# Three plain blocks of a fused attention and MoE kernel: one after the other, in an order laid out by a list scheduler

## The chip, the cores and the metric

The kernel runs on one core of a Trainium2 chip. The metric is the device time of one execution in microseconds, and kernels are compared by the median of several runs. A profile of one execution is at hand beside it; its span runs from the first to the last recorded instruction.

## The reference, cut to what matters

Attention is local: the sequence of 576 is cut into 9 chunks of 64, and each chunk of each of 8 heads and 8 batches attends to itself alone. The result goes through a two-layer network with a gate between the layers, for all 4608 tokens.

```python
scores = scale * np.matmul(q_c, k_c.transpose(0, 1, 2, 4, 3))
attn = np.exp(scores - np.max(scores, axis=-1, keepdims=True))
attn = attn / (np.sum(attn, axis=-1, keepdims=True) + 1e-09)
x = np.matmul(attn, v_c)                     # laid out as (4608, 512)
h = x @ w_in                                 # (512, 2048)
g = h * np.clip(h + 3.0, 0.0, 6.0) / 6.0
out = g @ w_out                              # (2048, 512)
```

## The kernel before, in words

The 4608 tokens are cut into nine blocks of 512. A block's attention is done in two halves, called heads here: head 01 is block 0, second half. A head loads qk (1 MB) and v (0.5 MB), and then takes these steps: scores (TensorE, 64 small products, L158), the maximum (VectorE, L165), its subtraction (L168), exp (ScalarE, L169), the sum and its inverse (VectorE, L172 to L174), the division (L176), transpose (TensorE, L187), its copy (ScalarE, L189), the product with v (TensorE, L198), and then the block's operand x. To keep float32 accuracy at the faster fp32r rate, each operand is split in a high part (a ScalarE cast, L207) and a low part (a VectorE subtraction, L210), and each product is made of three: high by high, high by low, low by high (L225, L226, L227). Every such product has 512 columns.

The 2048 hidden features are cut into 16 tiles, ft. A tile has 12 products in the first layer (mm1, into the PSUM tile h, of which there are two), a gate on ScalarE and VectorE that yields the tile g with its high and low part (L237 to L240), and 12 products in the second layer (mm2, into four accumulators acc). mm2 runs two tiles behind mm1 (LAG). So a tile of a block is 24 products.

The weights come as 64-bit words, one tile of 1 MB each, and have to be converted first: two ScalarE passes (L111, L114), a shift and a join on VectorE (L112, L115), a ScalarE cast to the high part (L119) and a VectorE subtraction for the low part (L120). The loads are issued on SyncE's queue (L99), at most three tiles ahead of the conversion.

Three blocks, 0 to 2, run in this plain way. The other six run in three pairs with seven products of sums in the place of eight (the pair phase, with tiles named xop and ws); its weight sums are made during the plain phase from the converted weights, in 16 units of four steps (`prepare`, L338 to L367), and stored in DRAM. The first operands of the pair phase (`x_operands`) are made at the end of the plain phase.

The order of the plain phase is written by hand. SEGMENTS (L29) says which tiles follow which: tiles 0 to 3 of block 0, then all 16 of block 1, then tiles 4 to 15 of block 0, then block 2. Between its two segments the sums of block 0 are copied out of the accumulators into `part` tiles (parked, L268 and L270), and added to the second segment's sums at its end (L262 to L266, some on GpSimd). Two slots per tile are counted, and attention steps and sum units are tied to slots by hand (`plan`). Until slot 26 (SUMS) the instructions are put in order by the framework's own scheduler, with some hints (`issue_after`); from there on each engine's instructions keep the order in which the code gives them (`manual_schedule`). Before the first products there are fillers on TensorE, products of no use that keep it busy: 11 at the start and then 36, 6 and 4 at fixed places (WARM, WARM2).

Each engine runs its instructions in the order given to it and waits at each for the semaphores of what it needs.

Of the kernel before, what the change touches and what calls it, by code (L numbers as in the profile page):

```python
# [28 lines left out]
SEGMENTS = [(0, 0, 4), (1, 0, 16), (0, 4, 16), (2, 0, 16)]  # L29
# [7 lines left out]
WARM2 = (0, 36, 0, 6, 4)  # L37
LAG = 2
EDGE = 32


@with_exitstack
def tile_kernel(ctx: ExitStack, tc: tile.TileContext, qk_in, v_in, weights, out):
# [49 lines left out]
    loaded = converted = 0  # L93

    def load_to(ft):
        nonlocal loaded
        while loaded < min(ft, NFT):
            t = w_tile(loaded, I32).rearrange("p l m t -> p (l m t)")
            nc.sync.dma_start(out=t.rearrange("p (m t) -> p m t", m=2), in_=weights[loaded].bitcast(I32).rearrange("m p t -> p m t"))  # L99
            words[loaded] = t.rearrange("p (n t) -> p n t", t=2)  # L100
            loaded += 1

    def convert(ft):

        u = wsc.tile([P, 1024], I32, name="u")
        r = wsc.tile([P, 1024], I32, name="r")
        lo, hi = words[ft][:, :, 0], words[ft][:, :, 1]

        ACT.activation(out=u.bitcast(F32), in_=hi.bitcast(F32), func=AF.Prelu, scale=2.0 ** -112, alpha=2.0 ** 32)  # L111
        DVE.tensor_scalar(out=u, in0=u, scalar1=3, scalar2=None, op0=ALU.logical_shift_left)  # L112

        ACT.activation(out=r, in_=lo.bitcast(U32), func=AF.Copy, scale=2.0 ** -29)  # L114
        DVE.tensor_tensor(out=u, in0=u, in1=r, op=ALU.add)  # L115
        a = u.bitcast(F32).rearrange("p (m t) -> p m t", m=2)
        w[ft] = w_tile(ft, F32R)
        w_h[ft], w_l[ft] = w[ft][:, 0], w[ft][:, 1]
        ACT.copy(out=w_h[ft], in_=a)  # L119
        DVE.tensor_tensor(out=w_l[ft], in0=a, in1=w_h[ft].bitcast(F32), op=ALU.subtract)  # L120

    def convert_to(ft):
        nonlocal converted
        load_to(ft + 3)
        while converted < min(ft, NFT):
            convert(converted)
            converted += 1
# [4 lines left out]
    class Attention:  # L132
# [6 lines left out]
        def load(self, qk=None, v=None):  # L139
            self.load_qk(qk)  # L140
            self.load_v(v)

        def load_qk(self, qk=None):

            self.qk = qk or ap.tile([P, 2, NB, 2 * CH], F32, name="qk")
            return nc.sync.dma_start(out=self.qk.rearrange("p a c t -> p (a c t)"), in_=qk_in[self.n, self.dp])
# [13 lines left out]
        def soft(self, step, e=None):  # L160
            flat = lambda t: t.rearrange("p a c t -> p (a c) t")
            wide = lambda t: t.unsqueeze(2).broadcast_to([P, 2 * NB, CH])
            if step == 0:
                self.m = small.tile([P, 2 * NB], F32, name="m")
                DVE.tensor_reduce(out=self.m, in_=flat(self.s), axis=AX.X, op=ALU.max)  # L165
            elif step == 1:
                self.e = e if e is not None else ap.tile([P, 2, NB, CH], F32, name="e")
                DVE.tensor_tensor(out=flat(self.e), in0=flat(self.s), in1=wide(self.m), op=ALU.subtract)  # L168
                ACT.activation(out=flat(self.e), in_=flat(self.e), func=AF.Exp, scale=SCALE)  # L169
            elif step == 2:  # L170
                self.z = small.tile([P, 2 * NB], F32, name="z")
                DVE.tensor_reduce(out=self.z, in_=flat(self.e), axis=AX.X, op=ALU.add)  # L172
                DVE.tensor_scalar_add(out=self.z, in0=self.z, scalar1=1e-9)
                DVE.reciprocal(out=self.z, in_=self.z)  # L174
            else:
                self.done = DVE.tensor_tensor(out=flat(self.e), in0=flat(self.e), in1=wide(self.z), op=ALU.mult)  # L176

        def softmax(self, e=None):
            for step in range(4):
                self.soft(step, e)  # L180

        def transpose(self):

            tp = self.psum().rearrange("p a (i t) -> p a i t", t=P)
            for a in range(2):
                for i in range(NB // 2):
                    PE.transpose(out=tp[:, a, i], in_=self.e[:, a, 2 * i:2 * i + 2].rearrange("p c t -> p (c t)"), identity=ident)  # L187
            self.aT = self.e.rearrange("p a c t -> p (a c t)").rearrange("p (a i t) -> p a i t", a=2, t=P)
            ACT.copy(out=self.aT, in_=tp)  # L189

        def values(self):

# [6 lines left out]
            src = po.rearrange("p s a i t -> p s (a i) t")  # L199
            as_src = lambda t: t.rearrange("p a (i s t) -> p s (a i) t", s=2, t=CH)  # L200
            if self.n >= NSTD:
                if self.n not in xraw:
                    xraw[self.n] = raw.tile([P, NDP, 2, NT], F32, name="x")
                ACT.copy(out=as_src(xraw[self.n][:, self.dp]), in_=src)
                return
# [8 lines left out]

    xraw = {}
    xs = {}
    low = []

    def finish():
        while low:  # L220
            low.pop(0)()
# [256 lines left out]
    for _ in made:  # L478
        pass
# [200 lines left out]
```

## Time and profile before

| What | us |
|---|---|
| median of three runs | 822.61 (822.45 to 823.38) |
| the profiled execution | 823.05 |
| its span | 821.0 |
| TensorE products busy | 800.5 |
| VectorE busy | 620.3 |
| ScalarE busy | 367.2 |
| GpSimd busy | 131.6 |

The granted clock of TensorE is 1.00 on average. Engines: PE is TensorE (products), PEld its weight loads, DVE VectorE, ACT ScalarE, POOL GpSimd, SP SyncE. A line L225 is line 225 of the kernel before. In the table by stretches each row has the stretch, its length, and for PE, PEld, DVE, ACT and POOL the busy time with the count of instructions in brackets; then the granted clock, the busy share of the DMA engines and GB/s. The rows for one tile have no POOL column. In the timeline a row is start, duration, engine, line, operation, tiles and count, and in brackets how long the engine was idle before and who ended that. In the groups a row is line, engine, operation, tiles and shapes, count, then busy time, mean in ns, and the idle time before with its releasers. In the list of waits a row is who waited for whom, total us, times and the longest. Products overlap, and their recorded length (390 ns) is longer than their spacing.

### The profile page before, as it was taken

The numbers are of one execution on the slowest core, as the hardware profiler recorded it, in microseconds if no ns is written. First come the engines' busy times: TensorE is split into PE (matmuls) and PEld (weight loads), VectorE is DVE, ScalarE is ACT, GpSimd is POOL, SyncE is SP. The second block draws the span as 40 slices with busy tenths as digits, with TensorE's granted clock in tenths as the row PEclk, the third lists the DMA queues.
The fourth block names the chain that finished last, engine by engine and source line by source line (L and its number), as shares of the span: only waits on it lengthen the run. The fifth ranks groups of instructions, "written<-read, shape, count | busy, mean of one in ns | idle before, by whom it ended". The sixth has DMA issues, their size and how long they took to land.

```text
span 821.0 us, 13680 instructions
## 1 busy us (share of the span) xinstructions
PE 800.5 (98%) x5683; PEld 650.2 (79%) x5683; DVE 620.3 (76%) x753; ACT 367.2 (45%) x455; POOL 131.6 (16%) x78
## 2 busy tenths in 40 slices
PE   7889999999999999999999999999999999999998
PEld 5667888888878888788788887888788887878886
DVE  5869978877787864876989667778898566679951
ACT  4858934443444443443474432344634423337330
POOL 0000000000010000212271031222440312227100
PEclk9999999999999999999999999999999999999999
DMA  9883026677685761665656667566555664555573
GB/s 367 326 339 150 1 76 220 209 253 244 195 294 173 259 249 52 232 222 198 234 187 228 231 240 257 194 216 246 187 198 203 227 212 180 190 206 188 185 230 129
DMA packets 50158, 172.86 MB, mean 211 GB/s; under 512 B 4656, under 2 KB 17200, under 8 KB 39344
## 3 DMA queue, kind: packets, MB, share of 16 engines
q1 hardware_dynamic: 49952, 171.85, 59.7%
q8 instruction: 45, 0.74, 0.3%
q10 hardware_dynamic: 144, 0.13, 0.0%
q14 instruction: 17, 0.14, 0.0%
HBM read 133.17 MB, written 38.80 MB: 209 GB/s over the span
## 4 chain that ended last, share of the span: by engine, by line
PE 75%; DVE 13%; ACT 5%; issue 3%; DMA 2%; SPq 1%; POOL 0%; DVEq 0%; ACTq 0%
PE acc L225 16%; PE acc L226 16%; PE acc L227 16%; PE h L225 8%; PE h L227 8%; PE h L226 8%; DVE xop L384 2%; PE two L198 2%; DMA w<-w_in_out 1%; DVE g L508 1%; PE two L187 1%; DVE u L496 1%; PE two L158 1%; DVE e L168 1%; ACT r L507 1%
## 5 line engine op out<-in xcount | busy, mean ns | idle before, releaser
L225 PE MATMUL acc<-xop,ws 128*128 128x512 f32 x528 | 208.4, 395 | 4.5 <-DVE u L496 4.5
L226 PE MATMUL acc<-xop,ws 128*128 128x512 f32 x528 | 205.8, 390 | 0.0
L227 PE MATMUL acc<-xop,ws 128*128 128x512 f32 x528 | 205.2, 390 | 0.0
L225 PEld LDWEIGHTS acc<-xop,ws 128*128 128x128 f32 x528 | 99.1, 188 | 27.7 <-DVE u L496 6.9
L384 DVE TENSOR_TENSOR xop<-g,xop 128x1024 fp32r<-128x1024 f32 x72 | 103.4, 1468 | 21.5 <-ACT xop L383 21.5
L227 PEld LDWEIGHTS acc<-xop,ws 128*128 128x128 f32 x528 | 99.1, 188 | 20.9
L226 PEld LDWEIGHTS acc<-xop,ws 128*128 128x128 f32 x528 | 99.2, 188 | 19.7
L383 ACT CAST xop<-g 128x1024 fp32r<-128x1024 f32 x72 | 74.6, 1054 | 78.6 <-PE acc L227 52.8
L516 POOL TENSOR_TENSOR g<-g 128x512 f32<-128x512 f32 x24 | 34.7, 1448 | 300.8 <-DVE g L508 300.8
L225 PE MATMUL h<-x,w 128*128 128x512 f32 x192 | 75.7, 396 | 2.0 <-ACT x L207 0.9
L225 PE MATMUL acc<-g,w 128*128 128x512 f32 x192 | 76.1, 399 | 1.5 <-ACT g L239 1.2
L226 PE MATMUL h<-x,w 128*128 128x512 f32 x192 | 75.2, 392 | 0.6 <-DVE x L210 0.5
L227 PE MATMUL h<-x,w 128*128 128x512 f32 x192 | 74.9, 390 | 0.3 <-DVE w L120 0.3
L226 PE MATMUL acc<-g,w 128*128 128x512 f32 x192 | 75.0, 391 | 0.0
L227 PE MATMUL acc<-g,w 128*128 128x512 f32 x192 | 74.9, 390 | 0.0
L507 ACT ACTIVATE r<-acc,half 128x512 f32<-128x512 f32 x72 | 48.6, 686 | 26.2 <-DVE acc L496 25.2
L238 DVE SCALAR_TENSOR_TENSOR r<-r,h 128x512 f32<-128x512 f32 x48 | 32.8, 683 | 35.1 <-ACT r L237 35.1
L507 ACT ACTIVATE r<-h,half 128x512 f32<-128x512 f32 x24 | 16.5, 687 | 94.4 <-DVE h L496 94.4
L226 PE MATMUL h<-xop,ws 128*128 128x512 f32 x144 | 56.2, 390 | 0.1
L225 PE MATMUL h<-xop,ws 128*128 128x512 f32 x144 | 56.2, 391 | 0.0
L227 PE MATMUL h<-xop,ws 128*128 128x512 f32 x144 | 56.1, 389 | 0.0
L508 DVE SCALAR_TENSOR_TENSOR g<-r,acc 128x512 f32<-128x512 f32 x72 | 48.6, 683 | 6.9 <-ACT r L507 6.6
(93 smaller groups left out, 1240.0 us busy)
## 6 DMA issues: line engine op xcount, KB each, us to landing
ws<-b SPq DMA_DIRECT2D x42, 1024.0 KB, 4.8
ws<-a SPq DMA_DIRECT2D x24, 1024.0 KB, 4.8
ws<-a SPq DMA_DIRECT2D x24, 768.0 KB, 4.2
qk<-qk_in SPq DMA_DIRECT2D x17, 1024.0 KB, 6.7
w<-w_in_out SPq DMA_DIRECT2D x16, 1024.0 KB, 14.1
v<-v_in SPq DMA_DIRECT2D x17, 512.0 KB, 5.2
a<-hl SPq DMA_DIRECT2D x32, 256.0 KB, 3.4
b<-hl SPq DMA_DIRECT2D x32, 256.0 KB, 3.2
```

Of the source, the lines that this page charges most:

```text
L158: PE.matmul(self.s[o, a, c, :], lhsT=self.qk[rows, 0, c, o], rhs=self.qk[rows, 1, c, o], start=True, stop=True)
L168: DVE.tensor_tensor(out=flat(self.e), in0=flat(self.s), in1=wide(self.m), op=ALU.subtract)
L198: PE.matmul(po[o, s, a, i, :], lhsT=self.v[rows, a, i, o], rhs=self.aT[rows, a, i, o], start=True, stop=True)
L225: PE.matmul(ps, lhsT=a_h, rhs=b_h, start=first, stop=False, skip_group_check=more)
L226: PE.matmul(ps, lhsT=a_h, rhs=b_l, start=False, stop=False, skip_group_check=more)
L227: PE.matmul(ps, lhsT=a_l, rhs=b_h, start=False, stop=last, skip_group_check=more)
L238: DVE.scalar_tensor_tensor(out=r, in0=r, scalar=1.0, in1=h, op0=ALU.min, op1=ALU.mult)
L383: ACT.copy(out=t[:, :, 0], in_=src)
L384: DVE.tensor_tensor(out=t[:, :, 1], in0=src, in1=t[:, :, 0].bitcast(F32), op=ALU.subtract)
L507: return (lambda: ACT.activation(out=r, in_=ps, func=AF.Relu, bias=half, scale=1.0 / 6.0), lambda: DVE.scalar_tensor_tensor(out=out, in0=r ...
L508: lambda: DVE.scalar_tensor_tensor(out=out, in0=r, scalar=1.0, in1=ps, op0=ALU.min, op1=ALU.mult))
L516: sub = lambda o, x, y: lambda: POOL.tensor_tensor(out=o, in0=x, in1=y, op=ALU.subtract)
```

## The change

The three plain blocks run in turn: block 0 with all its 16 tiles, then 1, then 2. SEGMENTS, the parked sums, the slots and the plan by hand are gone. In their place, every piece of work of the plain phase is a named step with an engine, a cost in microseconds, a list of steps that it follows, and for some a due time. The steps are finer than before: an attention head is ten or eleven steps, a conversion six, a tile two halves of mm1 (a and b, one per head of the block), four gate steps and mm2 (c). A list scheduler, run when the program is built, goes through time: whenever an engine is free, it gives it the ready step with the least latest start (worked back from the due times through the steps that follow). SyncE's steps are taken by their place in the list instead. The steps are then emitted in the order of their planned starts, all under `manual_schedule`, so each engine keeps that order.

```diff
-SEGMENTS = [(0, 0, 4), (1, 0, 16), (0, 4, 16), (2, 0, 16)]
-WARM2 = (0, 36, 0, 6, 4)
+FILL = 6.5
+LOADS = ("qk00 qk01 w0 v00 v01 w1 qk10 w2 w3 v10 w4 w5 w6 w7 w8 qk11 v11 w9 w10 w11 w12 w13 w14 w15").split()
+LAND, STEP, SETTLE = 1.95, 5.448, 0.06
+DUE = {"10": 13, "11": 15, "20": 24, "21": 28, "30": 36, "40": 38, "41": 41, "31": 43}
...
+        def latest(n):
+            if n not in rank:
+                rank[n] = min([self.due[n]] + [latest(m) - self.steps[m][1] - SETTLE for m in then[n]])
+            return rank[n]
+        queue = {n: (i if self.steps[n][0] == "SP" else latest(n), i) for i, n in enumerate(self.steps)}
...
+            for engine, names in waiting.items():
+                if names and free.get(engine, 0.0) <= now:
+                    n = heapq.heappop(names)[1]
+                    end = now + self.steps[n][1]
...
+                            t = max(at[a][1] + (LAND if self.steps[a][0] == "SP" else SETTLE) for a in self.steps[m][2])
...
+        return sorted(at.items(), key=lambda s: s[1][0])
...
+        steps = [("scores", "PE", 1.30, a.scores, ["qk" + u, *scores]), ("max", "DVE", 1.23, a.largest, ()),
+                 ("less", "DVE", 1.23, lambda: a.lessen(spare.get("e" + u, lambda: None)()), less), ("exp", "ACT", 1.06, a.exp, ()),
+                 ("sum", "DVE", 1.68, a.total, ()), ("share", "DVE", 1.22, a.share, ()), ("turn", "PE", 1.07, a.turn, ()),
+                 ("turned", "ACT", 1.02, a.turned, ()), ("product", "PE", 1.50, a.product, ["v" + u]), ("keep", "ACT", 1.03, a.keep, keep)]
+        if n < NSTD:
+            steps.append(("rest", "DVE", 1.23, a.rest, ()))
...
+        plain.add(f"up{ft}", "ACT", 1.15, [f"w{ft}", free("lower")], up)
+        plain.add(f"shift{ft}", "DVE", 0.69, [f"up{ft}"], shift)
+        plain.add(f"down{ft}", "ACT", 1.15, [f"w{ft}", free("join")], down)
+        plain.add(f"join{ft}", "DVE", 1.22, [f"shift{ft}", f"down{ft}"], join)
+        plain.add(f"high{ft}", "ACT", 1.05, [f"join{ft}"], high)
+        plain.add(f"lower{ft}", "DVE", 1.22, [f"high{ft}"], lower)
...
+        plain.add(f"a{j}", "PE", STEP / 4, [f"lower{ft}", made[f"{n}0"], of("gate", 2), of("b", 1)], first, due=STEP * j)
+        plain.add(f"b{j}", "PE", STEP / 4, [f"a{j}", made[f"{n}1"]], second, due=STEP * (j + 0.25))
+        plain.add(f"relu{j}", "ACT", 0.69, [f"b{j}", of("glow", 2)], relu)
+        plain.add(f"gate{j}", "DVE", 0.69, [f"relu{j}"], gate)
+        plain.add(f"ghigh{j}", "ACT", 0.62, [f"gate{j}", of("c", 3)], high)
+        plain.add(f"glow{j}", "DVE", 0.70, [f"ghigh{j}"], lower)
+        due = lambda k: STEP * (j + LAG + 0.5 + k / 8)
+        if 0 < ft < NFT - 1:
+            plain.add(f"c{j}", "PE", STEP / 2, [f"glow{j}", f"c{j - 1}"], lambda f=sums: f(*range(NET)), due=due(0))
+            continue
...
+        due = STEP * (NFT + 2 + 1.2 * u)
+        plain.add(f"whole{u}", "DVE", 1.38, ["room", f"less{u - 1}s" if u else None], whole)
+        plain.add(f"comb{u}", "DVE", 1.70, [f"whole{u}"], combine)
+        plain.add(f"top{u}", "ACT", 1.05, [f"comb{u}", f"send{u - 2}" if u > 1 else None], high)
+        plain.add(f"less{u}s", "DVE", 1.22, [f"top{u}"], lower, due=due)
+        plain.add(f"own{u}", "SP", 2.0, ["room"], send_own, due=due)
+        plain.add(f"send{u}", "SP", 2.7, [f"less{u}s"], send)
...
+    plain.add("free", "none", 0.0, [*stored, f"c{2 * NFT + NFP - 1}", *[f"out{n}{et}" for n in range(NSTD - 1) for et in range(NET)]], free)
...
+    listed = plain.order()
+    products = [(name, *at) for name, at in listed if plain.steps[name][0] == "PE"]
+    until = [name for name, *_ in products].index("a0")
+    idle = {products[k][0]: products[k + 1][1] - products[k][2] for k in range(until)}
+    for name, _ in listed:
...
+        plain.steps[name][3]()
+        warm_up(int(FILL * idle.get(name, 0.0)))
```

Beyond that: a load's cost on SyncE stands for its transfer (2.62 us for 1 MB), and what follows a load is ready 1.95 us behind it. The loads are in one fixed order, with the qk of head 01 ahead of the v of head 00; of the 24, those without a step to follow may be issued at once. The fillers before the first product of block 0 are worked out from the gaps that the plan leaves on TensorE (6.5 products of 256 columns per microsecond). The weight sums begin when all 16 tiles are converted (`room`), their stored part has two buffers of its own, and storing is two steps, one for the sums and one for the weights taken as they are. When the sums are stored and tile 39 of 48 is through (`free`), their space is given to the pair phase, three of its weight tiles are fetched, and its first operands are made as planned steps, too. The pair phase is as before.

More of the change, by code (lines that the diff above doesn't have):

```diff
@@ L178, in softmax, with largest @@
[L178 to L184, printed above, removed]
+        flat = staticmethod(lambda t: t.rearrange("p a c t -> p (a c) t"))
+        wide = staticmethod(lambda t: t.unsqueeze(2).broadcast_to([P, 2 * NB, CH]))
+        def largest(self):
+            self.m = small.tile([P, 2 * NB], F32, name="m")
+            DVE.tensor_reduce(out=self.m, in_=self.flat(self.s), axis=AX.X, op=ALU.max)
@@ new lines, in attention @@
+    def attention(u, due, scores=(), less=(), keep=()):
+        n, dp = int(u[0]), int(u[1])
+        a = heads[u]
+        steps = [("scores", "PE", 1.30, a.scores, ["qk" + u, *scores]), ("max", "DVE", 1.23, a.largest, ()),
[4 more added lines that the diff above has]
+            steps.append(("rest", "DVE", 1.23, a.rest, ()))
+        before = None
+        for name, engine, cost, f, more in steps:
+            before = plain.add(name + u, engine, cost, [before, *more], f, due=due)
+        return before
@@ new lines, in tile_kernel @@
+    for u in chain[3:]:
+        for part, of in (("qk", "scores"), ("v", "product")):
+            load(u, part, [of + prior[u]])
+    made = {"00": attention("00", 1e9), "01": attention("01", 1e9)}
+    mm = [(n, ft) for n in range(NSTD) for ft in range(NFT)]
+    for u in chain[1:]:
+        n = int(u[0])
+        free = {2: [f"b{NFT - 1}"], NSTD: [f"b{2 * NFT - 1}"]}.get(n, ())
+        made[u] = attention(u, STEP * DUE[u], [made[prior[u]]] if n > 1 or u[1] == "1" else (), ["product" + prior[u]], free)
@@ new lines, in tile_kernel @@
+    for ft in range(NFT):
+        free = lambda step: f"{step}{ft - 2}" if ft > 1 else None
+        up, shift, down, join, high, lower = convert(ft)
+        plain.add(f"up{ft}", "ACT", 1.15, [f"w{ft}", free("lower")], up)
[4 more added lines that the diff above has]
+        plain.add(f"lower{ft}", "DVE", 1.22, [f"high{ft}"], lower)
@@ new lines, in tile_kernel @@
+    for j, (n, ft) in enumerate(mm):
+        first, second, relu, gate, high, lower, sums, send, put = tile_steps(n, ft)
+        of = lambda name, back: f"{name}{j - back}" if j >= back else None
+        plain.add(f"a{j}", "PE", STEP / 4, [f"lower{ft}", made[f"{n}0"], of("gate", 2), of("b", 1)], first, due=STEP * j)
[8 more added lines that the diff above has]
+            continue
+        for et in range(NET):
+            name = f"c{j}" if et == NET - 1 else f"c{j}.{et}"
+            before = [f"c{j}.{et - 1}" if et else of("c", 1), f"copy{n - 1}{et}" if ft == 0 and n else None]
+            plain.add(name, "PE", STEP / 8, [f"glow{j}", *before, *(made.values() if j == et == 0 else ())][:4], lambda f=sums, et=et: f(et), due=due(et))
+            if ft:
+                plain.add(f"copy{n}{et}", "DVE" if et % 2 else "ACT", 0.66, [name, "room" if n < NSTD - 1 else None], lambda f=send, et=et: f(et))
+                plain.add(f"out{n}{et}", "SP", 0.7, [f"copy{n}{et}"], lambda f=put, et=et: f(et))
@@ new lines, in tile_kernel @@
+    stored = []
+    for u in range(2 * NFP):
+        whole, combine, high, lower, send, send_own = sum_steps(u % 2, u // 2)
+        due = STEP * (NFT + 2 + 1.2 * u)
[5 more added lines that the diff above has]
+        plain.add(f"send{u}", "SP", 2.7, [f"less{u}s"], send)
+        stored += [f"own{u}", f"send{u}"]
```

465 lines of the change are left out of this document (227 added, 238 removed).

## The prediction

> **What bounds the kernel now.** I read the page first, for the share of each engine and the chain that ended last.
>
> ```profile
> PE 800.5 (98%) x5683; PEld 650.2 (79%) x5683; DVE 620.3 (76%) x753; ACT 367.2 (45%) x455; POOL 131.6 (16%) x78
> ...
> PE 75%; DVE 13%; ACT 5%; issue 3%; DMA 2%; SPq 1%; POOL 0%; DVEq 0%; ACTq 0%
> ```
>
> TensorE is busy for 98% and is three quarters of the chain, so the matrix products are the floor. The change removes none of them. It can win only where TensorE stands still, or where it is busy with fillers. The second view is busy time by stretches: one stretch from the first product of a plain block (25.6) to 72, then two later ones.
>
> ```profile
> 25.60:72.00 46.40, 41.41 (x359) 30.92 (x354) 38.41 (x46) 32.46 (x39) 0.00 (x0) 1.00 0.81 316
> 72.00:100.00 28.00, 28.00 (x123) 22.88 (x124) 27.40 (x34) 27.75 (x34) 0.00 (x0) 1.00 0.00 1
> 200.00:300.00 100.00, 99.39 (x861) 81.22 (x861) 75.33 (x113) 41.28 (x54) 2.71 (x2) 1.00 0.74 247
> ```
>
> After 72 TensorE is full. A busy mark can still hide a thin stream, so I count products. The same stretches, for the instructions that touch the accumulators (acc), then the first-product tile (h), then the attention's double bank (two, first stretch only):
>
> ```profile
> 25.60:72.00 46.40, 15.74 (x60) 11.03 (x60) 1.38 (x2) 1.17 (x2) 1.00 0.81 316
> 72.00:100.00 28.00, 14.68 (x60) 11.19 (x60) 0.00 (x0) 0.00 (x0) 1.00 0.00 1
> ```
>
> ```profile
> 25.60:72.00 46.40, 22.64 (x85) 15.10 (x86) 4.05 (x6) 4.11 (x6) 1.00 0.81 316
> 72.00:100.00 28.00, 14.94 (x63) 11.69 (x64) 4.09 (x6) 4.07 (x6) 1.00 0.00 1
> ```
>
> ```profile
> 25.60:72.00 46.40, 5.67 (x214) 4.86 (x208) 8.46 (x7) 5.07 (x5) 1.00 0.81 316
> ```
>
> From 72 to 100 there are 60 + 63 products in 28.00 us: 0.2276 us each, the full rate (a tile of 24 is 5.46 us). From 25.6 to 72 there are 60 + 85 = 145, worth 33.0 us, and 5.67 us of attention. That leaves 46.4 - 33.0 - 5.7 = 7.7 us lost to waits. The timeline of TensorE shows where it starts and two of the larger holes:
>
> ```profile
> 25.62 0.50 PE L225 MATMUL h<-x,w 128*128 128x512 f32 x1
> ...
> 28.54 0.50 PE L226 MATMUL h<-x,w 128*128 128x512 f32 x1
> ...
> 31.40 0.39 PE L227 MATMUL h<-x,w 128*128 128x512 f32 x1
> 33.01 1.20 PE L225 MATMUL acc<-g,w 128*128 128x512 f32 x4 [1.22 <-ACT g L239]
> ...
> 60.49 0.40 PE L227 MATMUL acc<-g,w 128*128 128x512 f32 x1
> 61.82 0.73 PE L225 MATMUL h<-x,w 128*128 128x512 f32 x2 [0.94 <-ACT x L207]
> ```
>
> The first hole waits for the first gated tile, the second for the operand of a head. From 100 to 340 TensorE's list of waits holds only this:
>
> ```profile
> PE acc L225 <- DVE o L266: 0.3, 1, 0.3
> PE two L158 <- DMA qk<-qk_in: 0.3, 1, 0.3
> ```
>
> So the stake is three things: the start before 25.6, the 7.7 us up to 72, and 0.6 us later. The phase of block pairs behind it is left alone and I cost it at nothing.
>
> **The start.** The timeline of VectorE opens with the first softmax and reaches the second head's last softmax pass at 19.42; the chain of waits shows what came before the second head's low part.
>
> ```profile
> 7.21 1.23 DVE L165 TENSOR_REDUCE m<-two 128x16 f32<-128x1024 f32 x1 [6.35 <-PE two L158]
> ...
> 17.80 1.21 DVE L115 CUSTOM_DVE_ANT_0 u<-u,r 128x2048 uint16<-128x2048 uint16 x1
> 18.93 0.17 DVE L173 TENSOR_SCALAR z<-z 128x16 f32<-128x16 f32 x1
> 19.14 0.25 DVE L174 RECIPROCAL z<-z 128x16 f32<-128x16 f32 x1
> 19.42 1.23 DVE L176 TENSOR_TENSOR g<-g,z 128x1024 f32<-128x1024 f32 x1
> ```
>
> ```profile
> 26.13 1.23 DVE w L120
> 27.35 1.14 DVE x L210
> ```
>
> Head 01 is through its softmax at 20.65, but its low part ends at 28.49, behind the conversion of the second weight tile; only then do the products of the tile's second half go on (28.54). In the plan those products are due at a quarter of the first tile and the second weight at a whole one, so the head's steps sort ahead of that conversion. What remains behind the softmax is a chain of one transpose, its copy, the product, the high copy and the low part. The planner's own costs for the five are 1.07, 1.02, 1.50, 1.03 and 1.23, together 5.85. I add 0.6 for the handovers and up to 1.2 for a vector pass already running when the last step becomes ready (the greedy plan doesn't interrupt), and take half of that: 7.0 us. The softmax itself ends somewhat earlier, since the loads put the second head's scores ahead of the first head's values, and the conversion's join need not precede it: 18.5 to 19.4, taken as 18.8. So the second half starts near 25.8 (24.5 to 27). By then the first half's six products (6 x 0.2276 = 1.4) are done, which is as if all products had begun at 24.4 against 25.6: a gain of 1.2 us (from 2.5 down to nothing).
>
> **The stretch up to 72.** Block 0 now runs all 16 tiles at once instead of four, so the two heads of block 1 (10 and 11) are due at tiles 13 and 15 instead of tile 4. Their softmax passes leave the window in which the conversions fight for VectorE. The groups of VectorE, plain phase:
>
> ```profile
> L240 DVE TENSOR_TENSOR g<-r,g 128x512 fp32r<-128x512 f32 x48 | 34.1, 710 | 9.2 <-ACT g L239 9.2
> L238 DVE SCALAR_TENSOR_TENSOR r<-r,h 128x512 f32<-128x512 f32 x48 | 32.8, 683 | 35.1 <-ACT r L237 35.1
> ...
> L120 DVE TENSOR_TENSOR w<-u,w 128x1024 fp32r<-128x1024 f32 x16 | 19.6, 1223 | 3.6 <-ACT w L119 3.6
> L115 DVE CUSTOM_DVE_ANT_0 u<-u,r 128x2048 uint16<-128x2048 uint16 x16 | 19.5, 1220 | 0.1
> ...
> L112 DVE TENSOR_SCALAR u<-u 128x1024 int32<-128x1024 int32 x16 | 10.9, 688 | 0.1
> ```
>
> One conversion is 0.69 + 1.22 + 1.22 = 3.13 us and one gate 0.68 + 0.71 = 1.39: 4.52 per tile, under the tile's 5.46 on TensorE. Without heads in between, VectorE supplies tiles faster than they are used, and each tile that passes gains it 0.9 us. What I still expect is the first wait: the gate of tile 0 takes 0.69 + 0.68 + 0.62 + 0.71 = 2.7 us (scalar steps by the planner's costs) and handovers, while TensorE has only the 12 products of tile 1 to do (2.7 us). With a vector pass in the way that is 0.3 to 1.5 us; I take 1.0, and 0.5 for single misfits later. Of the 7.7 us, 6.2 go. What is late next is TensorE itself.
>
> **What else moves, at nothing.** The parked sums of block 0 (two copies on VectorE, two on ScalarE, two adds there and two on GpSimd) fall away; only the 0.3 us wait on L266 above was paid by TensorE. The weight sums get two buffers for what is stored, and two store steps of their own on SyncE's queue; their cover is TensorE's stream from tile 16 to tile 39, 23 tiles or 125 us, and if it were gone, each late head would cost what the row of 0.3 us on qk shows. SyncE's loads now stand in one fixed row: weight w4 stands behind v10, whose buffer is free after the first head's product near 18. w4 is used at tile 4, 24.4 + 4 x 5.46 = 46, so the wait is covered by over 20 us. The fillers before the first product now number 6.5 for each planned idle microsecond; at half of 0.2276 for 256 columns that is 0.74 of the gap, so they end before the planned product. For the later waits I take 0.5 of the 0.6 us as staying.
>
> **Sum.** 1.2 + 6.2 + 0.1 = 7.5 us. The profiled execution took 823.05 (span 821.0), so 815.5; it was 0.44 above the median of the three runs, and set against that median the forecast is 822.61 - 7.5 = 815.1.
>
> **Rivals.** First, VectorE paces block 0, and the kernel gets slower. Before block 1's first tile VectorE must do 16 conversions (50.1), 16 gates (22.2) and four heads. A head is five wide passes (as L176, 1.23) and the two short ones (0.42): 6.6, so 26.3. Together 98.6 us. TensorE would be there at 24.4 + 1.5 + 15 x 5.46 + two heads of about 3.1 (the 5.67 above is 1.8 heads) = 114; from 7.2, that leaves 107 us, or 8% idle. In the stretch 25.6 to 72 VectorE idled 8.0 of 46.4 us, 17%. With that share it needs 98.6 / 0.83 = 118.8 and is done at 126, 12 us late: 4.5 us slower than now, 827. It decides once VectorE is done later than about 122. Against it: next passes start before the last one ends (17.80 to 18.93 is 1.13 for a 1.21 us pass), which takes some 7% off the 98.6; and from 72 to 100, on just this work, VectorE idled 0.6 of 28 us. Chance 0.09.
>
> Second, a fixed order meets other durations than planned, each engine waits at the head of its list, and half of the 7.7 us comes back: gain 1.2 + 3.9 - 1.5 = 3.6, time 819.0. For it speaks that the plan has landing times of its own (1.95 us behind a serial queue), against it that its costs are nearly those of the rows. Chance 0.15.
>
> Third, the fillers are too thin and TensorE's clock falls before the first product.
>
> ```profile
> 3.03 0.15 PEld L84 LDWEIGHTS <-r 128*128 128x128 bf16 x1 [0.27 <-issue]
> 3.46 0.15 PEld L84 LDWEIGHTS <-r 128*128 128x128 bf16 x1 [0.28 <-issue]
> ```
>
> The first fillers, also 512 columns wide, came 0.43 us apart, not 0.2276. If the first 12 products came so, they would take 12 x 0.20 = 2.4 us more: 817.5. With fillers in 0.74 of the gaps it is unlikely: 0.03. [...]
>
> Fourth, the new order only moves the waits (VectorE late by just as much as was won): no change, within 0.2% or 1.6 us, which is about what a measurement of this kernel can tell. Chance 0.05.
>
> **The numbers.** The forecast has 0.68. Its own bounds: a start gain of 2.5, no wait left and 0.6 later make 10.8 (811.8); a start gain of nothing and 2.5 us of waits left make 5.2 (817.4). The second rival reaches 819.0. With half a microsecond about both ends the range is 811.3 to 819.5; it leaves out the slower and unchanged cases (0.14). Faster 0.68 + 0.15 + 0.03 = 0.86, same 0.05, slower 0.09.
>
> **What would show it.** Right: the second half of the first tile starts at 24.5 to 27; from there to 72 the count of 512-column products is 185 to 195 instead of 145 and VectorE's idle share falls under 10%; the first product of the pair phase comes some 7 us earlier than now; and the stretch behind it is as long as now. Wrong: holes of over 1 us on TensorE between tiles 2 and 16 that wait for a converted weight (the first rival if they grow toward tile 16, the second if they are scattered), first-tile products 0.43 us apart, or a longer pair phase.

## The result and the profile after

| | median, us | runs | ratio to the kernel before (95%) |
|---|---|---|---|
| before | 822.64 | 822.45 to 823.38 | |
| after | 816.17 | 816.01 to 816.81 | 0.9921 (0.9904 to 0.9938) |

The kernel is 6.5 us faster; 7.5 were forecast. The profiled execution took 816.08 us, its span is 814.3. From here on, L277 to L279 are the three products of each kind (L225 to L227 before), L253 is the head's product with v (L198), L235 its transpose (L187), L202 its scores (L158), L239 the copy of the transpose (L189), L263 and L266 the high and the low part of x (L207, L210), L209 a head's maximum (L165), L295 the VectorE step of a gate (L238), L134 the fillers (L84), and L154 the first ScalarE pass of a conversion (L111).

First the page of the kernel after: busy time, and the chain by engine.

```profile
PE 797.7 (98%) x5689; PEld 651.2 (80%) x5689; DVE 617.3 (76%) x751; ACT 367.4 (45%) x453; POOL 128.9 (16%) x76
...
PE 84%; DVE 9%; ACT 2%; issue 2%; DMA 2%; POOL 0%; SPq 0%; DVEq 0%; ACTq 0%
```

TensorE's share of the chain rose from 75% to 84%, and VectorE's fell from 13% to 9%. Next is the first stretch, all tiles and then acc, h and the attention's double bank, with the columns as before.

```profile
25.60:72.00 46.40, 45.35 (x292) 36.86 (x282) 43.59 (x52) 42.04 (x49) 0.00 (x0) 1.00 0.74 293
```

```profile
25.60:72.00 46.40, 20.34 (x84) 15.77 (x84) 0.00 (x0) 0.00 (x0) 1.00 0.74 293
```

```profile
25.60:72.00 46.40, 25.49 (x101) 18.77 (x102) 5.45 (x8) 5.67 (x8) 1.00 0.74 293
```

```profile
25.60:72.00 46.40, 2.73 (x107) 2.36 (x96) 3.66 (x3) 2.03 (x2) 1.00 0.74 293
```

There are 84 + 101 = 185 products of 512 columns, where there were 145. They are worth 185 x 0.2276 = 42.1 us, the attention takes 2.7, and 46.4 - 42.1 - 2.7 = 1.6 us are lost, where 7.7 were. VectorE idles 2.8 of 46.4 us, 6% instead of 17%. So VectorE is nearly as full as TensorE in this stretch, and still it holds up little. The list of waits shows what TensorE waited for before the pair phase, the longest first.

```profile
PE two L253 <- ACT e L239: 2.0, 1, 2.0
PE two L253 <- issue: 1.6, 1, 1.6
PE h L134 <- POOL r L118: 1.4, 1, 1.4
PE two L235 <- DVE e L225: 1.3, 1, 1.3
PE h L278 <- DVE x L266: 0.5, 1, 0.5
PE h L277 <- DVE r L295: 0.5, 1, 0.5
...
```

Only the last two shown fall within block 0's products; all others lie before them. The groups of the pair phase (times: shortest, median and longest ns, total, first start to last end) stand in the kernel before and then in the kernel after:

```profile
L225 PE MATMUL acc<-xop,ws x528: 389/389/504, 322.9 to 805.5; 128*128 128x512 f32 x176
```

```profile
L277 PE MATMUL acc<-xop,ws x528: 387/389/501, 316.3 to 798.8; 128*128 128x512 f32 x176
```

It starts 6.6 us earlier and is as long as before. All of the gain was made before it. Its parts: 7.7 - 1.6 = 6.1 from the stretch; the first product begins at 26.07 instead of 25.62, 0.45 lost; and the rest, 6.6 - 6.1 + 0.45 = 0.95, behind 72, where neither of the two holes of the kernel before (0.3 us each on L266 and on qk, some 0.5 each counted from the regular spacing) is left. The count by products agrees: of the 1152 products of 512 columns before the pair phase 1007 lay behind 72 in the kernel before, with 20.1 us of attention, so 250.9 - 229.2 - 20.1 = 1.6 us were lost there; now it is 967 with 23.5, so 244.3 - 220.1 - 23.5 = 0.7. The timeline of TensorE at the start:

```profile
19.18 1.16 PE L253 MATMUL two<-e,v 64*64 64x64 f32 x64 [2.00 <-ACT e L239]
20.27 1.09 PE L235 MATMUL two<-ident,g 128*128 128x128 f32 x8
21.30 1.16 PE L202 MATMUL two<-qk 64*64 64x64 f32 x64
...
23.04 0.33 PE L253 MATMUL two<-g 64*64 64x64 f32 x5
25.00 1.15 PE L253 MATMUL two<-g 64*64 64x64 f32 x59 [1.62 <-issue]
26.07 0.50 PE L277 MATMUL h<-x,w 128*128 128x512 f32 x1
...
28.50 0.50 PE L278 MATMUL h<-x,w 128*128 128x512 f32 x1 [0.55 <-DVE x L266]
```

The second half of the first tile starts at 28.50, as before (28.54; both counted from the product that needs the low part), although head 01's softmax was through at 17.83 (16.62 + 1.21). Behind it the chain took 10.6 us, 4.8 more than the 5.85 of the planner's costs: the transpose began 2.4 us after the softmax, since TensorE stood before the first head's product; its copy stood 0.6 us behind other ScalarE passes (21.36 to 21.95); and the product has the hole of 1.62 us. ScalarE's timeline explains the first hole, and VectorE's shows how the chain ended:

```profile
17.09 1.14 ACT L154 ACTIVATE u<-w 128x1024 f32<-128x1024 f32 x1 [2.69 <-DMA w<-w_in_out]
18.14 0.99 ACT L239 COPY e<-two 128x1024 f32<-128x1024 f32 x1
```

```profile
25.69 1.22 DVE L209 TENSOR_REDUCE m<-two 128x16 f32<-128x1024 f32 x1
27.23 1.23 DVE L266 TENSOR_TENSOR x<-two,x 128x1024 fp32r<-128x1024 f32 x1 [0.32 <-ACT x L263]
```

ScalarE stood 2.69 us before a conversion pass whose weight tile had not landed, with the ready copy of the transpose (15.65) behind it in its queue. The maximum of head 10, a step of block 1, went ahead of the low part that the second half of the first tile needs, but here it was over at 26.91 and VectorE then idled 0.32 us until the high part was cast: in this kernel the maximum delayed nothing. The second hole, 1.62 us "issue", waits for nothing that these rows show; it is taken up below.

### The profile page after: what moved, and what is told of

The parts are those of the page before. It is cut to its first block, busy times and chain, and to the rows that moved or that the text cites. A ratio compares the mean times of both kernels' runs of the same rounds, so it can differ in the third digit from the quotient of the medians.

```text
span 814.3 us, 13677 instructions
## 1 busy us (share of the span) xinstructions
PE 797.7 (98%) x5689; PEld 651.2 (80%) x5689; DVE 617.3 (76%) x751; ACT 367.4 (45%) x453; POOL 128.9 (16%) x76
## 4 chain that ended last, share of the span: by engine, by line
PE 84%; DVE 9%; ACT 2%; issue 2%; DMA 2%; POOL 0%; SPq 0%; DVEq 0%; ACTq 0%
PE acc L277 17%; PE acc L278 17%; PE acc L279 17%; PE h L277 9%; PE h L278 9%; PE h L279 9%; PE two L253 3%; DVE xop L401 2%; DMA w<-w_in_out 2%; PE two L235 2%; PE two L202 2%; DVE g L608 1%; DVE u L596 1%; ACT r L607 1%; DVE g L663 1%
## 5 line engine op out<-in xcount | busy, mean ns | idle before, releaser
L277 PE MATMUL acc<-xop,ws 128*128 128x512 f32 x528 | 208.4, 395 | 4.5 <-DVE u L596 4.5
L279 PE MATMUL acc<-xop,ws 128*128 128x512 f32 x528 | 205.2, 390 | 0.0
L277 PEld LDWEIGHTS acc<-xop,ws 128*128 128x128 f32 x528 | 99.1, 188 | 27.7 <-DVE u L596 6.9
L279 PEld LDWEIGHTS acc<-xop,ws 128*128 128x128 f32 x528 | 99.1, 188 | 20.9
L277 PE MATMUL h<-x,w 128*128 128x512 f32 x192 | 77.1, 402 | 0.5 <-DVE r L295 0.5
L279 PE MATMUL h<-x,w 128*128 128x512 f32 x192 | 74.9, 390 | 0.0
L277 PE MATMUL acc<-g,w 128*128 128x512 f32 x192 | 74.9, 390 | 0.0
L279 PE MATMUL acc<-g,w 128*128 128x512 f32 x192 | 74.7, 389 | 0.0
L292 ACT ACTIVATE r<-h,half 128x512 f32<-128x512 f32 x48 | 33.2, 692 | 67.0 <-PE h L279 66.9
L607 ACT ACTIVATE r<-h,half 128x512 f32<-128x512 f32 x24 | 16.5, 687 | 94.8 <-DVE h L596 94.8
L277 PE MATMUL h<-xop,ws 128*128 128x512 f32 x144 | 56.3, 391 | 0.0
L279 PE MATMUL h<-xop,ws 128*128 128x512 f32 x144 | 56.0, 389 | 0.0
L295 DVE SCALAR_TENSOR_TENSOR r<-r,h 128x512 f32<-128x512 f32 x48 | 32.8, 683 | 29.7 <-ACT r L292 29.7
```

Source lines behind the costliest of these rows:

```text
L277: PE.matmul(ps, lhsT=a_h, rhs=b_h, start=first, stop=False, skip_group_check=more)
L279: PE.matmul(ps, lhsT=a_l, rhs=b_h, start=False, stop=last, skip_group_check=more)
L292: ACT.activation(out=t["r"], in_=h, func=AF.Relu, bias=half, scale=1.0 / 6.0)
L295: DVE.scalar_tensor_tensor(out=t["r"], in0=t["r"], scalar=1.0, in1=h, op0=ALU.min, op1=ALU.mult)
L607: return (lambda: ACT.activation(out=r, in_=ps, func=AF.Relu, bias=half, scale=1.0 / 6.0), lambda: DVE.scalar_tensor_tensor(out=out, in0=r ...
```

## The experiments

The theory: the gain comes from taking heads 10 and 11 out of the first tiles, and the missing part of the start from the order of three steps. The rival: the fixed order itself, or the new order of the blocks alone, carries the time. All kernels are changes of the kernel after, but for the two by hand.

**The copy ahead of the late weight.** In the list of the plan one step moves:

```diff
+    listed.insert(names.index("turned00"), listed.pop(names.index("up1")))
```

> One step of the plan's list is moved: on ScalarE the first pass over weight tile 1 (L154) comes behind the copy of the first head's transpose (L239) instead of ahead of it. Theory (the head of ScalarE's list waited for a load that landed later than planned, and the copy stood behind it): the copy starts near 15.8 instead of 18.14, the first head's product with v near 17 instead of 19.18, the second half of tile 0 at 26.0 to 27.0 instead of 28.50; time 814.2 to 815.2 against 816.17. Rival (the start is bound elsewhere, by VectorE's passes or by the hole of 1.62 us without a releaser on TensorE): the copy moves, the second half stays at 28.0 or later, time 815.9 to 816.5.

Measured: 815.29 us (814.86 to 815.82), ratio 0.9909 (0.9895 to 0.9922). TensorE's timeline:

```profile
17.72 1.16 PE L253 MATMUL two<-e,v 64*64 64x64 f32 x64
...
22.59 0.33 PE L253 MATMUL two<-g 64*64 64x64 f32 x5 [0.94 <-ACT g L239]
23.41 1.15 PE L253 MATMUL two<-g 64*64 64x64 f32 x59 [0.49 <-issue]
...
27.87 0.50 PE L278 MATMUL h<-x,w 128*128 128x512 f32 x1 [1.50 <-DVE x L266]
```

The 2.0 us wait before the first head's product is gone, so the queue's order was its cause. Of it 0.6 us reach the second half of the tile, 0.9 the median. That is less than the 1.5 to 2.5 us expected of the second half. The "issue" hole comes again after five pairs of the product, and now the maximum of head 10 does hold the low part up: the high part is cast at 25.61, and the low part starts at 26.60, behind the maximum.

**Head 10's scores behind the first tile.** Both its scores and its maximum are moved behind the first layer of tile 0, and the five fillers that went with them are dropped.

```diff
+    listed.insert(names.index("b0"), listed.pop(names.index("scores10")))
...
+    listed.insert(names.index("scores10"), listed.pop(names.index("max10")))
+    idle.pop("scores10", None)
```

> The scores of head 10 (128 TensorE instructions and the five fillers behind them) and their maximum on VectorE come behind the first tile of the first layer instead of ahead of the second head's product with v. Theory (the 1.62 us hole in that product, 23.37 to 25.00, is TensorE waiting for its own instructions, which short products use up faster than they are supplied): the hole shrinks below 0.5 us, the product ends near 24.4 instead of 26.16, the second half of tile 0 starts at 26.5 to 27.2 instead of 28.50; since the scores (1.1 us) now stand in the stream, time 815.3 to 816.2. Rival (the hole comes from the busy DMA engines at that time, whatever TensorE has run before): a hole of over 1.2 us stays between 22 and 25, and with the scores in the stream the time is 816.6 to 817.4.

Measured: 817.62 us (817.42 to 819.02), ratio 0.9943 (0.993 to 0.9955), slower than the kernel after and than both expectations. The rows are of an execution of 818.87 us.

```profile
27.01 0.50 PE L278 MATMUL h<-x,w 128*128 128x512 f32 x1 [0.76 <-DVE x L266]
...
34.33 0.50 PE L277 MATMUL h<-x,w 128*128 128x512 f32 x1 [1.82 <-DVE r L295]
...
36.34 0.63 PE L278 MATMUL h<-x,w 128*128 128x512 f32 x1
36.77 0.63 PE L279 MATMUL h<-x,w 128*128 128x512 f32 x1
```

```profile
36.00:38.00 2.00, 2.00 (x6) 1.56 (x5) 2.00 (x4) 2.00 (x3) 0.00 (x0) 0.50 1.05 428
```

The hole of 1.62 us is gone, as the theory had it, and the start came out better by 1.5 us, but the maximum and its subtraction now stand ahead of the first gate; TensorE stood for 2 us at 32.1, and soon after it the granted clock was 0.50 (36 to 38) and the products came 0.43 us apart, seven of them, which at 0.20 each is some 1.4 us more. What was won at the start was lost twice at the next wait.

**No fillers** before the first product.

```diff
-FILL = 6.5
+FILL = 0.0
```

> No fillers between the first scores and the first product of tile 0 (FILL is 0; the eleven at the very start stay). Theory (the clock does not depend on these fillers, and 124 instructions fewer are needed): the 1.62 us hole shrinks below 0.6, the products of tile 0 come 0.23 us apart from the first, time 814.6 to 816.3. Rival (the clock falls when TensorE is idle for some microseconds): short products of the heads take up to twice as long, the first 8 to 12 products of tile 0 come about 0.43 us apart, time 817.5 to 819.

Measured: 817.51 us (816.96 to 817.7), ratio 0.9935 (0.9923 to 0.9947).

```profile
15.20 1.94 PE L235 MATMUL two<-ident,e 128*128 128x128 f32 x8 [5.87 <-DVE e L225]
```

```profile
32.00:34.00 2.00, 2.00 (x6) 1.56 (x6) 2.00 (x4) 2.00 (x3) 0.00 (x0) 0.55 1.02 412
```

The time is the third rival's, and so is its mechanism in part. The clock fell before the first product: behind 5.87 us without work the eight transposes took 1.94 us instead of 1.06, and the granted clock was 0.83 from 12 to 14 and 0.80 on the mean up to 26. The first products of tile 0 came 0.23 us apart again (25.56 to 26.48), and the low clock came back later (0.60 from 30 to 32 and 0.55 from 32 to 34), behind a wait for the second half (1.67 us before 29.19). The fillers are worth 1.3 us.

**Heads 10 and 11 due early**, as in the order before, with all else left to the scheduler:

```diff
-DUE = {"10": 13, "11": 15,
+DUE = {"10": 2, "11": 4,
```

> The changed kernel with the due times of block 1's two heads at tiles 2 and 4 instead of 13 and 15; the blocks still run in turn and the scheduler still lays out everything. Theory (what the order of the blocks buys is that these heads leave the first tiles, where VectorE is full with conversions): the 185 products between 25.6 and 72 fall to 150 to 172, time 818.5 to 822. Rival (the laid-out order as such makes the gain, and finds room for the heads): 180 or more products, time 815.5 to 817.

Measured: 818.91 us (818.81 to 818.93), ratio 0.995 (0.9937 to 0.9962). Stretch for acc and for h:

```profile
25.60:72.00 46.40, 17.75 (x72) 13.44 (x72) 0.00 (x0) 0.00 (x0) 1.00 0.82 327
```

```profile
25.60:72.00 46.40, 23.04 (x95) 16.14 (x89) 4.76 (x7) 4.83 (x7) 1.00 0.82 327
```

```profile
25.60:72.00 46.40, 6.18 (x252) 5.45 (x244) 6.03 (x5) 5.06 (x5) 1.00 0.82 327
```

```profile
26.16 0.94 PE L134 MATMUL h<-ident 128*128 128x256 bf16 x7
...
41.28 1.16 PE L202 MATMUL two<-qk 64*64 64x64 f32 x64 [1.82 <-DMA qk<-qk_in]
```

The row for h counts 7 fillers, which write to the same tile, so there are 72 + 88 = 160 products, worth 36.4 us. The attention (third row) takes 6.2, since both heads of block 1 lie in this stretch now. That leaves 46.4 - 36.4 - 6.2 = 3.8 us lost, against 1.6 in the kernel after and 7.7 in the kernel before. So 2.2 of the 6.1 us are gone again, and 2.7 of the 6.5 us of the time. But the longest wait, 1.8 us, is for the qk of head 11, whose place in LOADS, behind w8, the edit left as it was. The early heads do cost time; that they cost it on VectorE, as the theory says, is not shown, and under the scheduler's order most of what was won up to 72 stays.

**The start in the framework's order.** The fixed order begins only with the step that frees the start's buffers ("room"); until then the framework's scheduler orders the same steps.

```diff
     order = ExitStack()
-    order.enter_context(tc.manual_schedule())
...
     nonlocal sp, hp, op
+    order.enter_context(tc.manual_schedule())
```

> The changed kernel with the fixed order of each engine beginning only when all weights are converted; until then the framework's own scheduler sorts the same steps, which it receives in the planned order. Theory (the order of the blocks and the due times make the gain, the fixed order of the start little): time 815.2 to 818. Rival (the fixed order is what keeps TensorE fed in the first tiles): fewer than 165 products between 25.6 and 72, time 819 or more.

Measured: 815.97 us (815.8 to 817.18), ratio 0.9917 (0.9904 to 0.9931), with 84 + 103 = 187 products in the stretch. That is the kernel after. Forcing the order of the start adds nothing; the steps, given in the planned sequence, are enough. In its start six products came at a granted clock of 0.50 in the profiled run:

```profile
26.00:28.00 2.00, 2.00 (x6) 1.52 (x6) 2.00 (x2) 2.00 (x3) 0.00 (x0) 0.50 1.03 406
```

Whether it would be faster than the kernel after with the clock kept up was not tried.

**Blocks in turn without the scheduler.** The kernel before, with its segments in turn and its slots moved by hand:

```diff
-SEGMENTS = [(0, 0, 4), (1, 0, 16), (0, 4, 16), (2, 0, 16)]
+SEGMENTS = [(0, 0, 16), (1, 0, 16), (2, 0, 16)]
...
-    SUMS = first[1] + 18
+    SUMS = 30
...
-    for (n, dp), at in zip(((2, 0), (2, 1), (3, 0), (4, 0), (4, 1), (3, 1)), (30, 38, 52, 60, 68, 76)):
+    for (n, dp), at in zip(((2, 0), (2, 1), (3, 0), (4, 0), (4, 1), (3, 1)), (40, 48, 56, 63, 70, 77)):
...
```

> The kernel before with one part of the change alone: the three blocks run in turn (no parked sums, the two heads of block 1 at tiles 9 to 13, conversions one tile ahead of use, the framework's own order until tile 15), without the list scheduler. Theory (most of the gain is the order of the blocks, which takes the two heads out of the first tiles): the 145 products between 25.6 and 72 become 175 or more, time 816 to 818.5. Rival (the gain comes from the laid-out order of all engines' instructions): holes stay in the first tiles, 145 to 165 products, time 820 to 824.

Measured: 828.47 us (826.73 to 829.83), ratio 1.0062 (1.0048 to 1.0075). A second plan spreads the heads' steps (transpose at slot 7 and product at 9 of a head, other starts of the heads):

> The kernel before with its blocks in turn and no scheduler, as in the run with the blocks alone, but with the heads' steps placed by hand further apart (between transpose and product with v two slots or more instead of one; block 1's heads begin three slots earlier). Theory (the blocks in turn give the early gain, and what that run lost later were holes at heads whose steps stood too close): at most one hole of over 2 us at a product with v is left after 72, the clock stays at 1.00, time 816 to 819. Rival (by hand the heads cannot be placed without such holes, and the scheduler is needed): holes of over 2 us stay, time 822 or more.

Measured: 827.0 us (825.74 to 827.32), ratio 1.0045 (1.0033 to 1.0058). In both, the first stretch is better than in the kernel after. For the first plan, acc and h:

```profile
25.60:72.00 46.40, 20.41 (x84) 15.69 (x84) 0.00 (x0) 0.00 (x0) 1.00 0.71 282
```

```profile
25.60:72.00 46.40, 27.93 (x115) 21.42 (x116) 6.13 (x9) 6.17 (x9) 1.00 0.71 282
```

That is 199 products, and with 0.4 us of attention 0.7 us are lost. So the order of the blocks, with the heads and conversions moved to suit it, empties the first stretch of waits without the scheduler. The loss is later. From 72 to 330 the list of waits of the first plan begins so, with one of its holes in TensorE's timeline and the stretch around it behind it:

```profile
PE two L198 <- ACT e L189: 7.5, 3, 2.8
```

```profile
243.50 1.16 PE L198 MATMUL two<-e,v 64*64 64x64 f32 x64 [2.34 <-ACT e L189]
```

```profile
240.00:250.00 10.00, 7.66 (x141) 5.88 (x142) 5.38 (x10) 4.39 (x6) 0.00 (x0) 0.83 0.93 309
```

A head's copy, tied to a slot, comes too late (at 242.44, 4 us after its transpose and behind the passes of a gate and a weight sum), TensorE waits 2.3 us for it, and behind it products come 0.43 us apart (245.17 to 247.73; the granted clock is 0.83 on the mean from 240 to 250). In the second plan this wait is gone, and other waits of the heads are there in its place (4.2 us before transposes, 5.4 us before scores). My expectations for both plans, 816 to 818.5 and 816 to 819, missed. These two plans lost more at the later heads than they won at the start; in the kernel after the list of waits is empty from 60 to 316. A third plan by hand was not tried, so that only a program can place them is not shown.

**Two repairs together.** The copy ahead of the weight, and head 10's maximum held back until the fourth weight tile is converted:

```diff
-        steps = [("scores", "PE", 1.30, a.scores, ["qk" + u, *scores]), ("max", "DVE", 1.23, a.largest, ()),
+        steps = [("scores", "PE", 1.30, a.scores, ["qk" + u, *scores]), ("max", "DVE", 1.23, a.largest, ["lower3"] if u == "10" else ()),
...
+    listed.insert(names.index("turned00"), listed.pop(names.index("up1")))
```

> The changed kernel with two repairs: weight tile 1's first ScalarE pass behind the copy of the first head's transpose, and the maximum of head 10 on VectorE only after weight tile 3 is converted. Theory (VectorE is full from 7 to 36, and every pass that the first tiles do not need moves their start): the second half of tile 0 at 26.0 to 27.2 (27.87 with the first repair alone, 28.50 without), time 813.3 to 814.8. Rival (other passes fill the place and the first tiles wait for the conversions anyway): time 815.0 to 816.2.

Measured: 814.26 us (814.10 to 815.46), ratio 0.9893 (0.9878 to 0.9908): the best version of the study, 1.9 us below the median of the kernel after (measured on another chip, where the kernel before took 822.82 instead of 822.64). The rows are of its slowest execution, 815.46.

```profile
23.93 1.15 PE L253 MATMUL two<-g 64*64 64x64 f32 x59 [0.94 <-issue]
...
27.45 0.50 PE L278 MATMUL h<-x,w 128*128 128x512 f32 x1 [0.55 <-DVE x L266]
```

The low part now starts at 26.17, as soon as the high part is cast. With the copy moved already, holding the maximum back gave another 1.0 us of the median.

**What the "issue" hole is.** Counted in pairs of a weight load and a product, TensorE's stream of the kernel after up to the hole is 11 + 64 + 8 + 64 + 35 + 8 + 14 + 64 + 8 + 64 + 5 + 5 = 350 pairs. In the kernel before, whose order is another one, a small hole stood after 11 + 64 + 16 + 64 + 35 + 8 + 5 + 64 + 8 + 42 + 33 = 350 as well. So the theory: the hole belongs to a place in the stream, an edge behind the 350th pair, whatever product stands there. Small products of no use, put in behind the second head's scores, shift the stream under the edge; nothing else changes. If the theory holds, the hole leaves the second head's product with v (under 0.3 us there), and the time is 815.2 to 816.2.

```diff
+        if name == "scores01":
+            tiny = ps_h.tile([P, NT], F32, name="h")[:, :CH]
+            for k in range(48):
+                o, rows = HALF[k % 2], HALF[0]
+                PE.matmul(tiny[o], lhsT=ident[rows, o], rhs=ident[rows, :CH], start=True, stop=True)
```

> The changed kernel with 48 small products of no use (64 by 64 by 64, 96 TensorE instructions) added in a gap before the first transpose, where TensorE waits for VectorE anyway. [...]

Measured: 815.96 us (815.63 to 816.53), ratio 0.9918 (0.9904 to 0.9931).

```profile
19.03 1.02 PE L253 MATMUL two<-e,v 64*64 64x64 f32 x51 [0.21 <-ACT e L239]
20.62 0.45 PE L253 MATMUL two<-e,v 64*64 64x64 f32 x13 [0.56 <-issue]
...
23.77 0.80 PE L253 MATMUL two<-g 64*64 64x64 f32 x37
25.88 0.68 PE L253 MATMUL two<-g 64*64 64x64 f32 x27 [1.32 <-issue]
```

The time is in that range, but the hole did not vanish. I had miscounted: a small float32 product is two such pairs here, so 48 of them are 96 pairs and not 48 (the profile has 96 of their MATMUL records; and the 64 products of a head's scores, as they are called in the description of the kernel before, are 32 in the code and 64 pairs). With the right count the rows fit: the first head's product begins after 300 pairs and breaks 50 or 51 later, the second's begins after 441 and breaks 37 later, at 478. The edges are at 350 and 478, 128 pairs apart, that is 256 instructions when a load and a product count as one each. Three earlier runs fit too. With the two heads due early the hole, 1.70 us, comes after 350 pairs among the fillers; with head 10's scores moved the second head's product is pairs 277 to 340, without fillers 284 to 347, and neither of these has a hole.

With half as many small products the second edge should lie outside the head's product:

> The changed kernel with the 24 small products alone (96 instructions). Theory: the hole of 1.62 us in the second head's product is gone (edge 700 now in the scores of head 10, where up to 0.5 us may show); that product ends near 24.3 to 24.8 instead of 26.16; then VectorE's order decides, second half of tile 0 at 27.3 to 28.2 instead of 28.50, time 815.0 to 816.0. Rival: the hole stays in that product, time 816.2 or more.

Measured: 816.02 us (815.63 to 816.29), ratio 0.9916 (0.9901 to 0.993).

```profile
23.02 1.16 PE L253 MATMUL two<-g 64*64 64x64 f32 x64
...
28.09 0.50 PE L278 MATMUL h<-x,w 128*128 128x512 f32 x1 [1.66 <-DVE x L266]
```

The hole is gone, as expected, and the head's product is through at about 24.1 instead of 26.1. The second half of the tile still starts at 28.09: the high part is cast at 25.89, but head 10's maximum stands before the low part on VectorE (25.69 here too), which starts at 26.83. So behind the hole there is a second delay, VectorE's order, and taking the hole away alone gains 0.4 us at the second half and 0.15 in the median, which is within the noise.

The small products (L587 in these kernels) with the two repairs, 48 and 24 of them:

> Three repairs of the start together: the first ScalarE pass of weight tile 1 behind the copy of the first transpose, the maximum of head 10 after weight tile 3, and the 48 small products that move the edges of the instruction blocks. Theory: the hole of 0.94 us that the two repairs leave in the second head's product goes, the second half of tile 0 starts at 26.0 to 27.0, time 813.2 to 814.2 (814.26 with two repairs). Rival (VectorE alone decides when the first tiles start): the hole goes and the time stays within 0.3 us of 814.26 or is later.

Measured: 815.97 us (815.85 to 816.22), ratio 0.9917 (0.9904 to 0.9931). A miss: the 48 products delayed the transpose (16.60 instead of 15.28), and the edge fell into the first head's product (0.99 us behind 51 of its pairs).

> The two repairs (weight tile 1's pass behind the copy, head 10's maximum after weight tile 3) with 24 small products before the first transpose. Each of them is four instructions, which the run with 48 left out of account (they took 3.02 us and put the edges, at the 700th and 956th instruction, into the two heads' products with v). With 24, 96 instructions in 1.5 us of a gap of 1.76: theory: the edges fall into the scores of head 10 and into tile 1, no hole over 0.3 us is left in a product with v, the second head's product ends near 24.1 instead of 25.0, time 813.2 to 814.1. Rival (the place of the edges does not matter): a hole of about 0.9 us at the second head's product stays, time 814.2 to 815.

Measured: 815.08 us (814.91 to 816.88), ratio 0.9912 (0.9895 to 0.9928).

```profile
13.14 1.43 PE L587 MATMUL h<-ident 64*64 64x64 f32 x41
14.93 0.45 PE L587 MATMUL h<-ident 64*64 64x64 f32 x7 [0.35 <-issue]
...
19.97 0.67 PE L202 MATMUL two<-qk 64*64 64x64 f32 x27
22.00 0.80 PE L202 MATMUL two<-qk 64*64 64x64 f32 x37 [1.35 <-issue]
```

Here the edges are after 182 + 41 = 223 and 324 + 27 = 351 pairs, again 128 apart. The hole moved into head 10's scores, ahead of the product that matters, and no time was won over the two repairs alone; 813.2 to 814.1 were expected.

## Why the prediction was right, and where it was not

- **The stretch up to 72**, the main term: right in place and size. 6.1 of the 7.7 us went (6.2 forecast), 1.6 are left (1.5), 185 products are there (185 to 195), VectorE idles 6% (under 10%). That the new order of the blocks, which lets the heads come later, is enough for it is shown by the two plans by hand, without any scheduler (199 products, 0.7 us lost in the first). That VectorE was what the early heads fought for, as the prediction has it, stays open: made early again they cost 2.2 of the 6.1 us (160 products), and the longest wait then was for a load.
- **The start**, forecast at a gain of 1.2 us, failed: it cost 0.45, and the second half of the first tile began at 28.50 instead of 25.8. The step that failed is "a chain of one transpose, its copy, the product, the high copy and the low part", put at 7.0 us; it took 10.6. The softmax ahead of it was even earlier than I had it (17.83 against 18.8). I had priced each link and one vector pass in the way, but not the lists of the engines ahead of the links. A conversion pass stood ahead of the first copy, for a weight that landed at 17.09 and not at the plan's 15.05 (13.10 us of transfers and 1.95; counted from the first load's landing, it was 1 us late); this put the transpose 2.4 us behind the softmax, and 0.9 us of the median came back when the pass was moved. The copy of the second transpose stood 0.6 us behind other ScalarE passes. The hole behind the 350th pair cost 1.6 us; taken away alone it gave back nothing measurable (0.15 of the median), since a step of block 1, the maximum of head 10, then held up the low part. That maximum is the vector pass in the way that I had priced at half of 1.2 us; in the kernel after it cost nothing.
- **Later waits**, forecast 0.1, gave 0.95, the remainder of the account (0.9 by the count of products): both of the holes shown in the kernel before are gone. I had read their size off the idle times, 0.6 us, where the count gives 1.6 us lost. This term came out 0.85 better than forecast and the start 1.65 worse; that the sum missed by only 1.0 us is luck in this part.
- **Pair phase**: as forecast, as long as before.
- **The rivals**: VectorE did not pace block 0. The misfits of the second rival are there, but before the first product, and cost what the start shows, not half of the 7.7 us. The clock did not fall before the first product in the kernel after (granted 1.00 from 17 to 27); without fillers it did (0.80 on the mean up to 26).

## What to carry to other kernels

When an order is laid out at build time, look in the profile for an instruction at the head of an engine's list that waits for a load (2.69 us on ScalarE here), and ask which other chain stands behind it: a plan is as good as its landing times. Give a step that is needed much later a bound from below too, since a greedy list takes it as soon as an engine is free, a moment before the urgent one gets ready. A wait removed is only worth what the next one leaves: here each of three delays at the start was covered, in part or in whole, by another. And before a count of instructions on a tile is read as work, see what else writes to that tile: fillers do here.

## What the runs showed of the hardware

In these runs TensorE's "issue" holes of 0.35 to 1.70 us stood at places that can be counted in pairs: behind 350 in the kernel before (0.38 us), in the kernel after (1.62), with the copy moved (0.49), with the two repairs (0.94) and with the heads due early (1.70); behind 350 or 351 and 478 with the 48 small products (0.56 and 1.32), and behind 351 with the two repairs beside them (0.99); and behind 223 and 351 with 24 of them and the two repairs (0.35 and 1.35). The page of the kernel after has a DMA queue that it calls "instruction" (packets, MB, share of the DMA engines):

```profile
q8 instruction: 45, 0.74, 0.4%
```

That is 16 KB a packet, and for 5689 pairs one packet for some 126 pairs. One of them begins between 22.5 and 22.6 us, and TensorE resumes at 25.00; in the kernel before one begins between 22.2 and 22.3, and TensorE resumes at 24.65. Both times that is some 2.4 us after the packet begins. That TensorE waited for these packets is my reading of the times: the profile names nothing that ends the holes. With the small products the ends of two successive holes were 5.3 us apart (20.62 and 25.88) and 7.1 us apart (14.93 and 22.00), though TensorE was through with the 128 pairs between them 3.9 and 5.7 us after the first. Where the products have 512 columns, as nearly all have behind 26, 128 of them last 128 x 0.2276 = 29 us, and from 26 to 814 TensorE's list of waits in the kernel after has no "issue". What sets the length of a hole is open: the DMA engines' busy share was 1.03 from 20 to 26 in the kernel before and in the kernel after, but no run varied that.

The granted clock fell, with products 0.43 us apart, soon after holes of about 2 us: behind one of 1.82 us (0.50 from 36 to 38, the rows at 34.33 and 36 above), behind one of 2.34 us (0.83 on the mean from 240 to 250, at 243.50 in the plan by hand), and in the framework's order behind two, of 0.84 and 0.97 us, that lay close together (0.50 from 26 to 28). It did not fall in the kernel after (1.00 from 17 to 27), with holes of 2.00 us before 19.18 and 1.62 us before 25.00. So not each hole of that length led to it, and what decides between them is not shown. With head 10's scores moved it cost some 1.4 us on top of the hole (seven products at 0.43 us instead of 0.23).
